# Eight closing tiles whose sums move into DRAM writes, and a second opening row on GpSimd

## The chip, the cores and the metric

The kernel runs on one core of one Trainium2 chip. Its time is the device time of one execution in microseconds; the median of three executions of the kernel before is 1081.44 us (1080.97 to 1081.83). Engines are named as the profile names them: PE (matrix multiply), PEld (its weight loads), DVE (vector), ACT (scalar), POOL (GpSimd), SP (sync, here only an issuer of DMAs).

## The reference

For 2048 tokens of width D = 576 the kernel computes `out = u + s * g`, where

```
xn = layernorm(u)                                   # per token
s  = causal convolution of xn with K + xn * D_skip  # K from an S4D state-space model, by FFT
K  = 2 Re sum_n C_n dt exp(A_n dt l)
g  = silu( gelu( layernorm(xn) @ w1 + b1 ) @ w2 + b2 )   # hidden width F = 4608
```

Everything is float32. The convolution of length 2048 is done with small transform matrices on PE.

## The kernel before, in words

PE works almost without a break on the two large products of g. Each float32 operand is split in a high and a low part, and three products (high by high, high by low, low by high) replace one. The 2048 tokens fall in two halves of 1024; token tile b (0 to 15) holds 128 tokens, b, b+16, b+32 and so on. The hidden width goes in 12 groups of 384. One "slot" is one group on one block of 512 tokens: three products of layer 1 (line 519), then gelu on ACT (L552), the high part on ACT (L555), the low part on DVE (L558), then layer 2 (L577), whose result DVE adds into the accumulator `acc` (L585). The convolution's work is laid into the gaps by a planner (`Order`) that keeps a list of steps for each line of work and traces them by estimated durations; each engine then runs its instructions in the traced order.

**Opening.** Before the first slot the order is written by hand. Token tiles 0 to 3 ("rows" in what follows) are loaded in halves from SP and ACT (L344, L345). For each of the four rows `norms` gives the steps: statistics on DVE (L372, L374), two square roots on ACT (L378, L379), a reciprocal on DVE (L382; L1163 takes rows 2 and 3 together), and `second`, the subtract-and-scale into a tile named `row` (L394). Row 0 is scaled on POOL, rows 1 to 3 on DVE. PE runs dummy products meanwhile (`warm_up`, L1132), then turns each row by five transposes (`turn_row`, L421) into three PSUM tiles. When all four rows are turned, ACT copies the transposed blocks to `XH` (L425), DVE makes the low parts `XL` (L431), and PE's first real products begin (L534). ACT also issues the loads of b1 and of a small identity (L1146, L1147) and splits the first weights (L499); DVE and POOL make their low parts (L496).

**Closing.** Tiles 8 to 11 get their last layer-2 sum in the slot before last, tiles 12 to 15 in the last slot. Tile 15 goes in two halves of 288 columns. Early, SP has loaded u of tile k+8 into `TM[k]` (`last_x`) and s into `A` (`last_s`, L639); these are `x` and `s` of `finish`. For each tile `finish` adds four or three steps: ACT takes silu (tiles 12 to 15) or tanh (8 to 11) of `acc` (L653); DVE multiplies s by it (L658, or L660 and L664); DVE adds u (`total`, L668; in the trace `w<-w,A` or `v<-v,A`); two DMAs of 64 partitions each write the sum to `out` (L671). Both go from SP; for tiles 14 and 15 the second goes from ACT, and there it stands in ACT's own order between the silus. The results of the first half of the tokens (tiles 0 to 7) are combined on the way (`combine`, L616 to L628), with DMAs from POOL.

Of the kernel before, what the change touches and what calls it, by code (L numbers as in the profile page):

```python
# [9 lines left out]
F32 = mybir.dt.float32  # L10
# [3 lines left out]
OP = mybir.AluOpType  # L14
# [3 lines left out]
L, D, N, F = 2048, 576, 128, 4608  # L18
P = 128
# [19 lines left out]
TB = 512  # L39
# [3 lines left out]
def dve(n):  # L43
    return 0.075 + 0.00104 * n
# [163 lines left out]
def step(eng, dur, fn, need=(), mark=None, cv=0, at=0.0, late=0.0, tbl=None, by=1e9):  # L208
    return dict(eng=eng, dur=dur, fn=fn, need=tuple(need), mark=mark, cv=cv, at=at, late=late, tbl=tbl, by=by)
# [3 lines left out]
def mixer_kernel(ctx, tc, u, log_a_real, a_imag, c_real, c_imag, log_dt, d_skip, w1, b1, w2, b2,  # L213
# [8 lines left out]
    def bank2(name):  # L222
        return ps.tile([P, 2, TB], F32, name=name, bufs=2 if name == "cv" else 1)
# [250 lines left out]
    def split_raw(low_on=nc.vector):  # L474
        k = state["split"]
        state["split"] += 1
        half, g, which, i = PARTS[k]
        r = RAW.pop(k)
        if which == 1:
            if i == 0 and k:  # L480
                w1_tiles()
            h, lo, r1, r2 = W[1]
            if i < KB:
                h, lo = h[:, i], lo[:, i]
                m = P
            else:
                h, lo = r1, r2[:64]
                m = 64
        else:
            if i == 0:  # L490
                W[2] = (sb.tile([P, G, D], F32R, name="w2h"), sb.tile([P, G, D], F32R, name="w2l"))
            h, lo = W[2]
            h, lo, m = h[:, i], lo[:, i], P

        def low():
            low_on.tensor_sub(lo, r[:m], h[:m].bitcast(F32))  # L496
            for _ in range(NEXT[which - 1][i]):
                load_raw()
        nc.scalar.activation(h, r, AF.Copy)  # L499
        return low  # L500
# [135 lines left out]
    def last_s(k):  # L636

        m = A2F[:, k * D:(k + 1) * D]
        nc.sync.dma_start(m, s_s[:, 8 + k, :])  # L639
        XS[8 + k] = (TM[k], m)  # L640

    TM = []

    def finish(b, c0, c1, silu, end):

        c = slice(c0, c1)
        z = acc[:, b - 8, c]
        n = c1 - c0
        T = []

        def act_z():
            T.append(sb.tile([P, D], F32, name="row", bufs=NROW)[:, c])
            nc.scalar.activation(T[0], z, AF.Silu if silu else AF.Tanh, scale=1.0 if silu else 0.5)  # L653

        def mul():
            s = XS[b][1][:, c]
            if silu:
                nc.vector.scalar_tensor_tensor(s, s, 2.0, T[0], op0=OP.mult, op1=OP.mult)  # L658
            else:
                nc.vector.tensor_mul(s, s, z)  # L660

        def mul2():
            s = XS[b][1][:, c]
            nc.vector.scalar_tensor_tensor(s, T[0], 1.0, s, op0=OP.add, op1=OP.mult)  # L664

        def total():
            x, s = XS[b]
            nc.vector.tensor_add(x[:, c], x[:, c], s[:, c])  # L668
            for y, o in enumerate(rows_at(out, b, c.start, c.stop)):
                queue = nc.scalar if end and y else nc.sync  # L670
                queue.dma_start(o, x[64 * y:64 * y + 64, c])  # L671
        st = [step("ACT", act(n), act_z, tbl="silu" if silu else "gelu"), step("DVE", dve(n), mul)]
        if not silu:
            st.append(step("DVE", dve(n), mul2))
        return st + [step("DVE", dve(n), total)]


    def params():
# [445 lines left out]
    nc.gpsimd.memset(idp, 0.0)  # L1124
    for base in (0, 1 - P):
        nc.gpsimd.affine_select(idp, idp, [[2, P]], OP.not_equal, 1.0, base=base, channel_multiplier=-1)
    q0, q1, q2 = bank2("cv"), bank2("cv"), bank2("mxb")
    qb = bank2("mxa")

    def warm_up(n):  # L1130
        for _ in range(n):
            nc.tensor.matmul(qb[:, 0], zero[:, :P], zero, start=True, stop=True)  # L1132
# [2 lines left out]
    w1_tiles()  # L1135
    na[0][0](0)

    b1r = sb.tile([P, TB], F32, name="h32", bufs=2)[:F // P, :P]
    tr = [y_transpose(0, 0, k, q) for k, q in enumerate((q0[:, 0], q1[:, 0], q2[:, 0], q0[:, 1], q1[:, 1]))]

    def turn_row(i):
        for k in (0, 3, 1, 4, 2):
            tr[k][0](i)
    lows = []
    na[0][1]()
    nc.scalar.dma_start(b1r, b1.rearrange("(k p) -> k p", p=P))  # L1146
    nc.scalar.dma_start(idt, ident)  # L1147
    na[0][2]()
    na[0][3](0, nc.gpsimd)
    turn_row(0)  # L1150
    warm_up(2)
    na[1][0](0)
    na[1][1]()
    na[2][0](0)
    lows.append(split_raw(nc.vector))
    na[2][1]()
    na[3][0](0)
    lows.append(split_raw(nc.vector))
    na[3][1]()
    na[1][2]()  # L1160
    na[1][3](0)
    turn_row(1)
    nc.vector.reciprocal(PAIR[3], PAIR[3])  # L1163
    for b in (2, 3):
        na[b][3](0)
        turn_row(b)
    nc.tensor.transpose(q2[:, 1, :F // P], b1r, idt[:F // P, :F // P])
    lows += [split_raw(nc.gpsimd), split_raw(nc.gpsimd)]
    lows[0]()
# [314 lines left out]
    for slot in range(NSLOT):  # L1484
        turn[0] = slot + 1
        n, g, tb = SEQ[slot]
        change = slot + 1 < NSLOT and SEQ[slot + 1][0] != n
        final = slot >= NSLOT - 2
        for pos in range(NPOS):
            if pos < G:  # L1490
                need = wmark(n, 1) + [("x", tb)]
                if pos == 0:
                    if slot in (mid, mid + 1):
                        x_ready(tb)
                    od.force(lambda: all(m in od.marks for m in need))

                    if slot in (3, 2 * NG + 1):
                        od.marks["x", tb] -= 2.3
                cell = []
                od.unit(lambda: cell.extend([layer1(g, tb, pos)] if slot else first_layer1(pos)),  # L1500
                        L1 if slot else L1 * (22, 6, 14)[pos] / 14, need)
                look_ahead(pos)
                for k, (a, b, c) in enumerate(cell, pos + 1 - len(cell)):
                    by = hidden_by(pos, k)
                    od.urgent.append((od.t["PE"], [step("ACT", 0.62, a, tbl="gelu", by=by[0]),
                                                   step("ACT", act(TB), b, by=by[1]),
                                                   step("DVE", dve(TB), c, mark=("h", slot, k), by=by[2])]))
                od.advance(od.t["PE"])
                if pos == G - 1 and change:
                    weigh_in(1)  # L1510
            else:
                j, terms, last, hid = l2_terms(pos - G)
                need = [wmark(n, 2)[i] for i in hid] + [("h", slot, i) for i in hid]
                if pos == G:

                    pe_turns()
                od.force(lambda: all(m in od.marks for m in need))
                if max(od.marks[m] for m in need) > od.t["PE"] + 0.3:
                    pe_turns(any_time=True)
                cell = []  # L1520
                halves = slot == NSLOT - 1 and j == 3
                od.unit(lambda: cell.append(layer2(g, tb, j, terms, last, halves)), LEN[pos], need)
                look_ahead(pos)
                if last or halves:
                    add = cell[0]
                    dh, k = (terms[0][1], 1) if halves else (0, 2)
                    done = ("acc", slot, j, dh)
                    chain = [step("DVE", dve(288 * k), lambda: add(dh, k), mark=done, by=add_by(pos, j))]
                    if final:
                        b = 8 + 4 * tb + j  # L1530
                        x = el if slot < NSLOT - 1 else od.line()
                        st = finish(b, dh * 288, (dh + k) * 288, slot == NSLOT - 1, slot == NSLOT - 1 and j > 1)
                        st[0]["need"] = (done, ("s8", b - 8))
                        x["steps"] += st
                    elif slot in GATE:
                        for d in range(2):
                            one, two = gate_store(4 * tb + j, d)
                            by = od.t["PE"] + 5.0
                            chain += [step("ACT", act(288), one, tbl="gelu", by=by), step("DVE", dve(288), two, by=by)]
                    od.urgent.append((od.t["PE"], chain))  # L1540
                if pos == NPOS - 1 and change:
                    weigh_in(2)
            for f in LATER.get((slot, pos), ()):
                f()
            od.advance(od.t["PE"])
            pe_turns(all_lines=pos in (0, 1, G + 1, G + 3, G + 5, NPOS - 1))
# [55 lines left out]
```

## Time and profile before

| | us |
|---|---|
| median of three executions | 1081.44 |
| the profiled execution's own time | 1081.68 |
| its span, first to last instruction | 1079.90 |
| first real product of PE begins (L534) | 12.95 |
| last product of PE ends (L577) | 1072.77 |
| last DVE sum ends (L668) | 1076.55 |

The profiled execution lies 0.24 us above the median, and 1.78 us of its time lie outside the span. A timeline row gives start, duration, engine, line, operation, `out<-in` by the program's tile names, shapes, and in brackets the idle time before it with the engine that ended it; `xN` merges N instructions of a kind, whose duration is then that of the whole stretch. PE's granted clock is 0.998 of full speed over the span.

### The profile page before, as it was taken

To read this page: it belongs to the slowest core of one execution; us is meant where nothing else is said; L and a number is where in the kernel's file an instruction comes from. 1 tells how busy PE (TensorE), PEld (TensorE's weight loads), DVE (VectorE), ACT (ScalarE), POOL (GpSimd) and SP (SyncE) were. 2 spreads that over 40 slices of the span, in tenths; PEclk is the share of its full clock that TensorE was granted. 3 is DMA by queue.
4 is the path that set the end of the run, shared out by engine and by line. 5 is a ranking of instruction groups with operands and counts; after the bars stand their busy time and mean duration, and the time that the engine had idled before them with its cause. 6 is when DMAs were issued, how large, how long until landed. Compare 5 with 4: busy or idle time off the path is not lost.

```text
span 1079.9 us, 27247 instructions
## 1 busy us (share of the span) xinstructions
PE 1070.8 (99%) x11471; PEld 932.4 (86%) x11471; DVE 955.2 (88%) x1535; ACT 662.2 (61%) x985; POOL 211.0 (20%) x304
## 2 busy tenths in 40 slices
PE   9999999999999999999999999999999999999997
PEld 7989899888888888888888887898888888888896
DVE  7789878999999999999999999999999997668367
ACT  6656768877658575686657657566667655234233
POOL 5669433111100020000200002000200013011231
PEclk9999999999999999999999999999999999999999
DMA  7885456643224141457322244133322436343434
GB/s 233 236 261 184 145 180 213 197 109 131 65 76 120 30 128 52 107 148 147 89 62 77 65 85 118 32 107 51 103 59 85 125 60 229 98 132 98 128 117 121
DMA packets 138570, 129.71 MB, mean 120 GB/s; under 512 B 88636, under 2 KB 109216, under 8 KB 137424
## 3 DMA queue, kind: packets, MB, share of 16 engines
q1 hardware_dynamic: 121792, 78.31, 26.8%
q0 software_dynamic: 15904, 48.70, 14.6%
q8 instruction: 90, 1.47, 0.6%
q10 hardware_dynamic: 752, 0.97, 0.3%
q14 instruction: 32, 0.26, 0.1%
HBM read 98.50 MB, written 35.19 MB: 124 GB/s over the span
## 4 chain that ended last, share of the span: by engine, by line
PE 96%; DVE 3%; issue 1%; ACT 0%; POOL 0%; ACTq 0%; DVEq 0%; POOLq 0%
PE mxb L577 21%; PE mxa L577 21%; PE mxa L519 21%; PE mxb L519 20%; PE cv L881 3%; PE cv L991 3%; PE cv L1044 2%; PE cv L953 2%; PE cv L1071 1%; PE mxa L1132 1%; DVE w2l L496 0%; PE mxa L534 0%; DVE pr L720 0%; DVE hl L558 0%; DVE A L658 0%
## 5 line engine op out<-in xcount | busy, mean ns | idle before, releaser
L577 PE MATMUL mxa<-w2h,hh 128*128 128x288 f32 x573 | 171.3, 299 | 0.3 <-DVE acc L585 0.3
L577 PE MATMUL mxb<-w2h,hh 128*128 128x288 f32 x576 | 171.6, 298 | 0.0
L577 PE MATMUL mxb<-w2h,hl 128*128 128x288 f32 x576 | 170.2, 296 | 0.0
L577 PE MATMUL mxb<-w2l,hh 128*128 128x288 f32 x576 | 169.5, 294 | 0.0
L577 PE MATMUL mxa<-w2h,hl 128*128 128x288 f32 x573 | 169.4, 296 | 0.2 <-DVE hl L558 0.2
L577 PE MATMUL mxa<-w2l,hh 128*128 128x288 f32 x573 | 168.7, 294 | 0.0
L558 DVE TENSOR_TENSOR hl<-h,hh 128x512 fp32r<-128x512 f32 x144 | 99.2, 690 | 65.2 <-ACT hh L555 64.7
L552 ACT ACTIVATE h<-mxa,b1t 128x512 f32<-128x512 f32 x73 | 50.3, 690 | 120.8 <-PE mxa L519 119.8
L781 POOL DMA_DIRECT2D par<-par_s x36 | 27.4, 762 | 480.4 <-DVE mg L824 436.4
L577 PEld LDWEIGHTS mxa<-w2h,hh 128*128 128x128 f32 x573 | 107.6, 188 | 9.8 <-issue 4.7
L577 PEld LDWEIGHTS mxb<-w2h,hh 128*128 128x128 f32 x576 | 108.1, 188 | 7.7 <-issue 3.0
L577 PEld LDWEIGHTS mxb<-w2l,hh 128*128 128x128 f32 x576 | 108.1, 188 | 0.6
L577 PEld LDWEIGHTS mxb<-w2h,hl 128*128 128x128 f32 x576 | 108.1, 188 | 0.4 <-DVE hl L558 0.2
L577 PEld LDWEIGHTS mxa<-w2h,hl 128*128 128x128 f32 x573 | 107.5, 188 | 0.6 <-DVE hl L558 0.6
L577 PEld LDWEIGHTS mxa<-w2l,hh 128*128 128x128 f32 x573 | 107.6, 188 | 0.5
L552 ACT ACTIVATE h<-mxb,b1t 128x512 f32<-128x512 f32 x71 | 49.0, 690 | 74.0 <-PE mxb L519 73.3
L555 ACT ACTIVATE hh<-h 128x512 fp32r<-128x512 f32 x144 | 91.2, 634 | 4.2
L585 DVE TENSOR_TENSOR acc<-mxa,acc 128x576 f32<-128x576 f32 x88 | 65.7, 746 | 21.3 <-PE mxa L577 20.8
L519 PE MATMUL mxa<-XH,w1h 128*128 128x512 f32 x284 | 78.9, 400 | 0.0
L519 PE MATMUL mxb<-XH,w1h 128*128 128x512 f32 x280 | 77.5, 398 | 0.0
L519 PE MATMUL mxa<-XL,w1h 128*128 128x512 f32 x284 | 76.2, 390 | 0.0
L519 PE MATMUL mxa<-XH,w1l 128*128 128x512 f32 x284 | 76.0, 389 | 0.0
(239 smaller groups left out, 2450.9 us busy)
## 6 DMA issues: line engine op xcount, KB each, us to landing
raw<-in_B_w_dram SPq DMA_DIRECT2D x75, 288.0 KB, 3.3
raw<-in_B_w_dram SPq DMA_DIRECT2D x100, 192.0 KB, 3.4
par_s<-A POOLq DMA_DIRECT2D x8, 1080.0 KB, 5.2
par<-par_s POOLq DMA_DIRECT2D x36, 240.0 KB, 3.4
f2t<-f2q SPq DMA_DIRECT2D x24, 256.0 KB, 3.5
raw<-in_B_w_dram SPq DMA_DIRECT2D x50, 96.0 KB, 3.6
u_s<-in_A_u_dram POOLq DMA_DIRECT2D x16, 288.0 KB, 4.8
xc<-xn_s SPq DMA_DIRECT2D x48, 96.0 KB, 3.8
```

Source lines behind the costliest of these rows:

```text
L519: nc.tensor.matmul(q, a, b, start=j == 0, stop=j == len(ops) - 1)
L552: nc.scalar.activation(t, q, AF.Gelu_apprx_tanh, bias=b1t[:, g * G + i:g * G + i + 1], scale=1.0)
L555: LAST[0] = nc.scalar.activation(hh[:, i], t, AF.Copy)
L558: nc.vector.tensor_sub(hl[:, i], t, hh[:, i].bitcast(F32))
L577: nc.tensor.matmul(q[:, dh, :288], a[:, i, c], b[:, i, d], start=i == 0 and k == 0, stop=i == G - 1 and k == 2)
L585: nc.vector.tensor_add(o, q[:, dh:dh + n, :288], b if first else o)
L781: nc.gpsimd.dma_start(PAR[b].rearrange("p (g i) k -> p g (i k)", g=4), dram(par_s, (b // 6 * CH + b % 6 * 4) * NPAR, [[D * NPAR, P], [24 * ...
L881: nc.tensor.matmul(q[32 * g:32 * g + 32, i // 2, i % 2 * 64:i % 2 * 64 + 64], U[:, ri, 4 * g + i, :], v[:, ri, 4 * g + i, :], start=ri == ...
L953: nc.tensor.matmul(Q1ST[i, x][g // 2][64 * f:64 * f + 64, g % 2].rearrange(order), f1t[r].rearrange("p s k -> p (s k)"), rhs(r, f), start= ...
L991: nc.tensor.matmul(Q[i][32 * q:32 * q + 32, f, 2 * ri:2 * ri + 2], m[r, 4 * i + q, 32 * ri:32 * ri + 32], A2[r, 4 * p + 2 * i + q // 2, :, ...
L1044: nc.tensor.matmul(QI[q // 2][64 * f:64 * f + 64, q % 2, i], MAT["g2t", p + i // 2][r, i % 2, ri], YS[p + i // 2][0][r, i % 2, ri, f], sta ...
L1071: nc.tensor.matmul(Q[f][32 * e:32 * e + 32, t], g1t[r], A2[r, k:k + 2, 1].rearrange("p i d r -> p i r d"), start=True, stop=True, skip_gro ...
```

## The change

The sum of tiles 8 to 14 leaves DVE. SP writes u of the tile from `TM[k]` to `out` as soon as s has been loaded, two DMAs a tile (14 in all). The last product of a tile (`product`) now writes over the u tile in SBUF, and POOL issues two DMAs that add it to what `out` holds (`accum_op`). Seven of DVE's nine sums are gone. Tile 15 keeps its two sums; ACT issues only the last of its four stores, where ACT issued three of the six stores of tiles 14 and 15 before. A new condition (`need`) puts the first half's product of tile 15 behind the sum of the second half into `acc`.

In the opening POOL scales row 1 too, right after row 0; the reciprocals of rows 2 and 3 are separate; rows are turned in the order 0, 2, 1, 3; one dummy product instead of two stands after row 0. POOL issues the loads of b1 and of the identity, now 36 by 36 instead of 128 by 128, ahead of its scalings.

```
         nc.sync.dma_start(m, s_s[:, 8 + k, :])
         XS[8 + k] = (TM[k], m)
+        if k < 7:
+            for y, o in enumerate(rows_at(out, 8 + k, 0, D)):
+                nc.sync.dma_start(o, TM[k][64 * y:64 * y + 64])
...
+        def product(a, k, op, b2):
+            x, s = XS[b]
+            o = s[:, c] if end else x[:, c]
+            nc.vector.scalar_tensor_tensor(o, a, k, b2, op0=op, op1=OP.mult)
+            if not end:
+                for y, r in enumerate(rows_at(out, b, c0, c1)):
+                    nc.gpsimd.dma_start(r, o[64 * y:64 * y + 64], accum_op=OP.add)
...
-                queue = nc.scalar if end and y else nc.sync
+                queue = nc.scalar if c1 == D and y else nc.sync
...
-        return st + [step("DVE", dve(n), total)]
+        return st + [step("DVE", dve(n), total)] * end
...
+    nc.gpsimd.dma_start(b1r, b1.rearrange("(k p) -> k p", p=P))
+    nc.gpsimd.dma_start(idt[:F // P, :F // P], ident[:F // P, :F // P])
...
-    nc.scalar.dma_start(b1r, b1.rearrange("(k p) -> k p", p=P))
-    nc.scalar.dma_start(idt, ident)
     na[0][2]()
     na[0][3](0, nc.gpsimd)
     turn_row(0)
-    warm_up(2)
+    warm_up(1)
...
+    na[1][2]()
+    na[1][3](0, nc.gpsimd)
...
-    na[1][3](0)
-    turn_row(1)
-    nc.vector.reciprocal(PAIR[3], PAIR[3])
-    for b in (2, 3):
-        na[b][3](0)
-        turn_row(b)
+    na[2][2]()
+    na[2][3](0)
+    turn_row(2)
+    turn_row(1)
+    na[3][2]()
+    na[3][3](0)
+    turn_row(3)
...
-                        st = finish(b, dh * 288, (dh + k) * 288, slot == NSLOT - 1, slot == NSLOT - 1 and j > 1)
+                        st = finish(b, dh * 288, (dh + k) * 288, slot == NSLOT - 1, slot == NSLOT - 1 and j == 3)
                         st[0]["need"] = (done, ("s8", b - 8))
+                        if halves and not dh:
+                            st[1]["need"] = (("acc", slot, j, 1),)
```

The order on DVE in the opening, from the reciprocal of row 0 to the first weight split, stood so before:

```order
L382 RECIPROCAL U_88<-U_88 128x2
L372 BN_STATS st_171<-acc_87 128x6 x2
L374 BN_AGGR U_88<-st_171 128x2
L372 BN_STATS st_177<-acc_87 128x6 x2
L374 BN_AGGR U_88<-st_177 128x2
L372 BN_STATS st_184<-acc_87 128x6 x2
L374 BN_AGGR U_88<-st_184 128x2
L382 RECIPROCAL U_88<-U_88 128x2
L394 TENSOR_SCALAR row_192<-acc_87,U_88 128x576
L1163 RECIPROCAL U_88<-U_88 128x2x2
L394 TENSOR_SCALAR row_200<-acc_87,U_88 128x576
L394 TENSOR_SCALAR row_207<-acc_87,U_88 128x576
```

and stands so now (`st_...` of the second, third and fourth statistics are rows 1, 2 and 3):

```order
L382 RECIPROCAL U_88<-U_88 128x2
L372 BN_STATS st_170<-acc_87 128x6 x2
L374 BN_AGGR U_88<-st_170 128x2
L372 BN_STATS st_176<-acc_87 128x6 x2
L374 BN_AGGR U_88<-st_176 128x2
L382 RECIPROCAL U_88<-U_88 128x2
L372 BN_STATS st_186<-acc_87 128x6 x2
L374 BN_AGGR U_88<-st_186 128x2
L382 RECIPROCAL U_88<-U_88 128x2
L394 TENSOR_SCALAR row_194<-acc_87,U_88 128x576
L382 RECIPROCAL U_88<-U_88 128x2
L394 TENSOR_SCALAR row_207<-acc_87,U_88 128x576
```

The reciprocal of row 1 moved ahead of row 3's statistics, and one scaling of three left DVE (POOL has it behind row 0's).

The order on DVE at the end, from the sum of tile 12 into `acc`, stood so before (`w` and `v` are u tiles, `A_81` the s tiles, `cv` the last half of tile 15):

```order
L585 TENSOR_TENSOR acc<-mxb,acc 128x576
L585 TENSOR_TENSOR acc<-mxa,acc 128x576
L658 SCALAR_TENSOR_TENSOR A_81<-A_81,row 128x576
L668 TENSOR_TENSOR w<-w,A_81 128x576
...
L585 TENSOR_TENSOR acc<-mxb,acc 128x576
L668 TENSOR_TENSOR w<-w,A_81 128x576
L585 TENSOR_TENSOR acc<-mxa,acc 128x288
L658 SCALAR_TENSOR_TENSOR A_81<-A_81,row 128x576
L585 TENSOR_TENSOR acc<-cv,acc 128x288
L668 TENSOR_TENSOR v<-v,A_81 128x576
L658 SCALAR_TENSOR_TENSOR A_81<-A_81,row 128x288
L668 TENSOR_TENSOR v<-v,A_81 128x288
...
```

and stands so now (L661 is the product, L678 the sum that is left):

```order
L585 TENSOR_TENSOR acc<-mxb,acc 128x576
L585 TENSOR_TENSOR acc<-mxa,acc 128x576
L661 SCALAR_TENSOR_TENSOR w<-A_81,row 128x576 x2
L585 TENSOR_TENSOR acc<-mxb,acc 128x576
L585 TENSOR_TENSOR acc<-mxa,acc 128x288
L661 SCALAR_TENSOR_TENSOR v<-A_81,row 128x576
L585 TENSOR_TENSOR acc<-cv,acc 128x288
L661 SCALAR_TENSOR_TENSOR A_81<-A_81,row 128x288
L678 TENSOR_TENSOR v<-v,A_81 128x288
...
```

The three sums of 576 columns are gone; a product and a sum of 288 columns follow twice after the last sum from `cv`.

The end of ACT's order, from the silu of tile 12, stood so before:

```order
L653 ACT_TABLE_LOAD
L653 ACTIVATE row<-acc 128x576 x3
L653 ACTIVATE row<-acc 128x288
L671 DMA out_dram<-v 64x576
L653 ACTIVATE row<-acc 128x288
L671 DMA out_dram<-v 64x288 x2
```

and stands so now:

```order
L656 ACT_TABLE_LOAD
L656 ACTIVATE row<-acc 128x576 x3
L656 ACTIVATE row<-acc 128x288 x2
L681 DMA out_dram<-v 64x288
```

No DMA stands between the last two silus any more.

## Rows read from the trace of the kernel before

**Rows 1.** Page: the chain of work that ended last, by engine.
```profile
PE 96%; DVE 3%; issue 1%; ACT 0%; POOL 0%; ACTq 0%; DVEq 0%; POOLq 0%
```

**Rows 2.** Timeline of the last stretch, PE and ACT: start, duration, instruction.
```profile
1070.11 0.30 PE L577 MATMUL mxb<-w2h,hl 128*128 128x288 f32 x1
...
1071.65 0.69 ACT L653 ACTIVATE row<-acc 128x576 f32<-128x576 f32 x1 [2.11 <-DVE acc L585]
...
1072.48 0.29 PE L577 MATMUL cv<-w2h,hl 128*128 128x288 f32 x1
...
1074.38 0.54 ACTq L671 DMA_DIRECT2D out_dram<-v  x1
...
1075.12 0.45 ACT L653 ACTIVATE row<-acc 128x288 f32<-128x288 f32 x1 [1.93 <-DVE A L658]
```

**Rows 3.** Timeline of the last stretch, DVE.
```profile
1070.86 0.75 DVE L585 TENSOR_TENSOR acc<-mxb,acc 128x576 f32<-128x576 f32 x1
...
1072.20 0.45 DVE L585 TENSOR_TENSOR acc<-mxa,acc 128x288 f32<-128x288 f32 x1
1072.56 0.75 DVE L658 SCALAR_TENSOR_TENSOR A<-A,row 128x576 f32<-128x576 f32 x1
1073.23 0.45 DVE L585 TENSOR_TENSOR acc<-cv,acc 128x288 f32<-128x288 f32 x1
...
1075.60 0.46 DVE L658 SCALAR_TENSOR_TENSOR A<-A,row 128x288 f32<-128x288 f32 x1 [0.39 <-ACT row L653]
1076.09 0.46 DVE L668 TENSOR_TENSOR v<-v,A 128x288 f32<-128x288 f32 x1
```

**Rows 4.** Line L671: SP's last issues (ns min/median/max, first and last start); landing.
```profile
L671 SPq DMA_DIRECT2D out_dram<-v x3: 467/467/468, 1074.4 to 1076.6; - x3
...
DMA to landing us min/median/max: 2.0/2.4/3.5
```

**Rows 5.** Timeline of the opening, DVE.
```profile
5.79 0.17 DVE L382 RECIPROCAL U<-U 128x2 f32<-128x2 f32 x1 [0.55 <-ACT U L379]
...
7.36 0.82 DVE L372 BATCH_NORM_STATS2 st<-acc 128x6 f32<-128x288 f32 x2 [0.21 <-DMA acc<-in_A_u_dram]
8.21 0.21 DVE L374 BATCH_NORM_AGGREGATE U<-st 128x2 f32<-128x12 f32 x1
...
10.64 1.07 DVE L394 TENSOR_SCALAR row<-acc,U 128x576 f32<-128x576 f32 x2
```

**Rows 6.** Timeline of the opening, POOL, PE and ACT.
```profile
6.07 2.29 POOL L394 TENSOR_SCALAR row<-acc,U 128x576 f32<-128x576 f32 x1 [3.93 <-DVE U L382]
...
11.33 0.60 PE L421 MATMUL cv<-idp,row 128*128 128x128 f32 x4
...
11.88 0.60 PE L421 MATMUL cv<-idp,row 128*128 128x128 f32 x4
...
12.30 1.09 ACT L425 ACTIVATE XH<-cv 128x512 fp32r<-128x512 f32 x2 [1.07 <-PE cv L421]
```

**Rows 7.** Timeline of the last stretch, POOL: its last four issues.
```profile
1066.73 2.13 POOL L628 DMA_DIRECT2D out_dram<-row  x4 [10.92 <-DVE row L625]
```

**Rows 8.** Page: POOL's loads from DRAM; KB each, us to landing.
```profile
par<-par_s POOLq DMA_DIRECT2D x36, 240.0 KB, 3.4
```

**Rows 9.** Line L404: landing of POOL's stores of a whole row tile.
```profile
DMA to landing us min/median/max: 2.4/3.5/6.6
```

**Rows 10.** Timeline of the last weight load (SP) and its slot's first layer-2 product.
```profile
1030.28 0.33 SPq L459 DMA_DIRECT2D raw<-in_B_w_dram  x1
...
1044.03 0.29 PE L577 MATMUL mxa<-w2h,hh 128*128 128x288 f32 x1
```

**Rows 11.** Timeline around 88 us: a POOL scaling beside DVE scalings.
```profile
86.54 0.57 DVE L394 TENSOR_SCALAR row<-w,U 128x576 f32<-128x576 f32 x1
...
86.81 2.80 POOL L403 TENSOR_SCALAR w<-w,U 128x576 f32<-128x576 f32 x1
...
88.03 1.06 DVE L394 TENSOR_SCALAR row<-v,U 128x576 f32<-128x576 f32 x2
```

More of the change, by code (lines that the diff above doesn't have):

```diff
@@ L657, in mul @@
             if silu:
-                nc.vector.scalar_tensor_tensor(s, s, 2.0, T[0], op0=OP.mult, op1=OP.mult)
+                product(s, 2.0, OP.mult, T[0])
             else:
@@ L662, in mul2 @@
         def mul2():
-            s = XS[b][1][:, c]
-            nc.vector.scalar_tensor_tensor(s, T[0], 1.0, s, op0=OP.add, op1=OP.mult)
+            product(T[0], 1.0, OP.add, XS[b][1][:, c])
         def total():
@@ L1126, in mixer_kernel @@
         nc.gpsimd.affine_select(idp, idp, [[2, P]], OP.not_equal, 1.0, base=base, channel_multiplier=-1)
+    b1r = sb.tile([P, TB], F32, name="h32", bufs=2)[:F // P, :P]
+    nc.gpsimd.dma_start(b1r, b1.rearrange("(k p) -> k p", p=P))
+    nc.gpsimd.dma_start(idt[:F // P, :F // P], ident[:F // P, :F // P])
     q0, q1, q2 = bank2("cv"), bank2("cv"), bank2("mxb")
@@ L1136, in mixer_kernel @@
     na[0][0](0)
-    b1r = sb.tile([P, TB], F32, name="h32", bufs=2)[:F // P, :P]
     tr = [y_transpose(0, 0, k, q) for k, q in enumerate((q0[:, 0], q1[:, 0], q2[:, 0], q0[:, 1], q1[:, 1]))]
@@ L1154, in mixer_kernel @@
     na[2][0](0)
+    na[2][1]()
+    na[1][2]()
+    na[1][3](0, nc.gpsimd)
     lows.append(split_raw(nc.vector))
-    na[2][1]()
     na[3][0](0)
+    na[3][1]()
     lows.append(split_raw(nc.vector))
-    na[3][1]()
-    na[1][2]()
-    na[1][3](0)
+    na[2][2]()
+    na[2][3](0)
+    turn_row(2)
     turn_row(1)
-    nc.vector.reciprocal(PAIR[3], PAIR[3])
-    for b in (2, 3):
-        na[b][3](0)
-        turn_row(b)
+    na[3][2]()
+    na[3][3](0)
+    turn_row(3)
     nc.tensor.transpose(q2[:, 1, :F // P], b1r, idt[:F // P, :F // P])
```

## The prediction

> **What bounds the kernel now.** I read the chain of work that ended last first: 96% of it is PE [rows 1]. From its first real product to its last, which ends at 1072.48 + 0.29 = 1072.77 [rows 2], PE is the whole chain, and the change leaves the products as they are. So only the two ends can change the time: what happens before the first product, and the 1079.90 - 1072.77 = 7.13 us behind the last. For these I read the timelines, engine by engine.
>
> At the end the reader is to see two queues that are late [rows 2, 3]. The last bank is full at 1072.77, but DVE turns to it at 1073.23, since it has been in tile 14's product from 1072.56. DVE is done with it at 1073.68, yet the silu of that half starts on ACT only at 1075.12: in ACT's order the store of tile 14 stands ahead, and this waits for DVE's sum and goes at 1074.38. The product follows at 1075.60, the sum at 1076.09 to 1076.55. From there to the end of the span it is 3.35 us: the issues start at 1076.6, a store lands 2.4 us after its issue starts [rows 4], and about 0.9 us close the program.
>
> In the opening the last transpose counts. Row 3 is scaled at the end of the pair 10.64 to 11.71 [rows 5], PE begins to turn it at 11.88, 0.55 after row 2, ACT copies from 12.30 [rows 6], and PE's first real product waits for that copy.
>
> **The end, part by part.** The sums of tiles 12, 13 and 14 go from DVE, and with them the ACT store. Each step below uses gaps of these rows: a product started 0.36 after an independent instruction of 288 columns (1072.20 to 1072.56), a sum 0.49 after its product (1075.60 to 1076.09), ACT 0.04 after DVE (1070.86 + 0.75 to 1071.65) [rows 2, 3]; I take 0.04 between the other engines too. PE's pace is (1072.48 - 1070.11) / 18 = 0.132 per product.
>
> - Tile 14's bank is full at 1070.41. DVE, which stood in tile 13's product until 1070.86, is free: sum into `acc` 1070.45 to 1071.20, silu 1071.24 to 1071.93, product 1071.97 to 1072.72. The bank of tile 15's first half is full nine products before the end, at 1071.58; its sum runs at 1071.62, its silu 1072.11 to 1072.56.
> - DVE is then free for the last bank: 1072.81 to 1073.26, and silu 1073.30 to 1073.75, without the store ahead of it.
> - DVE goes on with the first half's product at 1073.17, sum 1073.66 to 1074.12, the second half's product at 1074.02 (0.36 after the sum's start; its silu is ready), sum 1074.51 to 1074.97. This is 1.58 before 1076.55.
> - ACT's store starts at once. SP has the first half's two stores ahead of its last one: issues of 0.47 from 1074.15, so the last starts at 1075.09 or a little after where it was 1076.6: 1.46 earlier by 1075.12. SP's store is the later of the two, so the end gains **1.46**.
>
> What stands against it are POOL's additions. Tiles 12 and 13 are done in time; tile 14's product ends at 1072.72, POOL issues in 2.13 / 4 = 0.53 each [rows 7], the second from 1073.30. No row shows an adding DMA. It can land no sooner than the fastest store, 2.0 [rows 4], and with a load and a store one behind the other, 3.4 [rows 8] + 2.4 = 5.8; the longest landing of a plain store of POOL is 6.6 [rows 9]. Hidden is what lands within 4.2 us: 1073.30 + 4.2 + 0.9 = 1078.4, where the other stores end too (1074.97 + 3.35 + 0.12). I take 3.5, the median of POOL's stores of a tile twice this size, so it costs nothing.
>
> SP's 14 early stores of u follow its loads of s, the first twelve of them ahead of the last weight load. With about 0.5 an issue they push it by 6 us; it went at 1030.28, and PE first uses its group at 1044.03 [rows 10], so 13.7 us cover it, less its landing and its split. On POOL four additions of tiles 8 and 9 push the last loads of tiles 6 and 7 by 2.1, and four of tiles 10 and 11 follow; POOL then idled 10.92 us [rows 7], which covers both. The tanh of tile 10 now waits for POOL's stores of tiles 3 to 5, and the gelu behind it on ACT is needed only three layer-1 products later.
>
> **The opening, part by part.** DVE loses one scaling (0.5), and row 3 is ready sooner: reciprocal of row 1 behind row 2's statistics (8.42), row 3's statistics end about 9.65, row 2 scaled 9.8 to 10.4, reciprocal, row 3 scaled 10.5 to 11.1 in place of 11.71. But row 1 is now POOL's. Row 2's statistics wait for their data until 7.36 and end at 8.42; the reciprocal 8.45 to 8.62 [rows 5]; POOL follows 0.11 after it, as 5.96 to 6.07 for row 0. POOL's scaling takes 2.29 with nothing beside it [rows 6], so row 1 is ready at 8.73 + 2.29 = 11.02. Beside DVE's scalings it took 2.80: it began at 86.81, one DVE scaling ran until 87.11 and two from 88.03 [rows 11]. That is 0.51 for two and a part, 0.2 each. Here two fall into it, so 11.02 + 0.40 = 11.42.
>
> PE begins to turn a row 0.11 after it is ready (10.64 + 0.58 to 11.33); row 3 comes 0.55 after row 1; ACT 0.42 after that [rows 6]: 11.42 + 0.11 + 0.55 + 0.42 = 12.50 where it was 12.30. So the opening **loses 0.20**, and what follows shifts as a whole, since it hangs on that copy. Bounds: without the stretch 12.10, a gain of 0.20; with the full 0.51 12.61, a loss of 0.31. ACT's two issues go and its roots come sooner, which is worth nothing, since ACT idles 1.07 us ahead of 12.30 [rows 6]. POOL's two issues lie in the 3.93 us in which it waited for row 0 [rows 6]. The dummy product that goes lay ahead of row 1's turn and frees nothing now.
>
> **Sum.** 1081.68 - 1.46 + 0.20 = 1080.42 for an execution like the profiled one; the median lies 0.24 lower: **1080.2 us**.
>
> **The rivals.**
>
> *POOL is not slowed.* Row 1 at 11.02, the opening gains 0.20: 1079.8. For it: bn_stats beside row 0 cost POOL nothing (2.29). Against it: the 2.80 of [rows 11].
>
> *The additions land last (the other side).* If an addition reads what `out` holds before it writes, it lands after 5.8 us: 1073.30 + 5.8 + 0.9 = 1080.0, against 1079.90 before, and with 0.20 of the opening 1081.8: slower by 0.3, with 6.6 us by 1.1 (1082.6). It decides from 4.2 us on, and it makes the kernel slower from 5.5. For it: loads take longer than stores, and an addition is both. Against it: the data is small, and reading and writing may overlap across its 64 rows. The Trainium skill ("Collectives: The Full Stack", section "The bandwidth ceiling: the fold count and why AG ≠ RS ≠ AR") says that an add in the DMA path is slow because it reads two sources, not because of the add; no run here shows it yet.
>
> *DVE waits for POOL.* If POOL's scaling, which starts first, held DVE's two scalings back until 11.02, row 2 would be ready at 11.60 and row 3, with its reciprocal, at 12.3; the copy comes at 12.3 + 0.11 + 0.42 = 12.85, a loss of 0.55: 1080.5. In [rows 11] DVE's pair took 1.06 though POOL had begun 1.2 us before, as 1.07 in the opening with POOL idle [rows 5], and it was POOL that took longer. The Trainium skill ("SBUF — State Buffer", section "Who interferes with whom") says that the engine which issues first holds the shared pair of ports for its whole instruction and the other blocks; by that rule this rival would be the forecast, and the trace does not agree.
>
> **How the numbers follow.** Forecast 56%, POOL not slowed 15%, additions last 18% (in a third of it slower than before), DVE waits 6%, something I do not see 5%. The forecast's own range is 1079.7 to 1080.8. The range for 8 in 10 takes the gain of both ends at its best (-1.58 - 0.20, less 0.3 for the scatter of the executions: 1079.3) and the addition at 5.8: 1079.3 to 1081.8. A measurement can tell about 0.2%, 2.2 us, from no change. All my cases but the worst additions lie within it: faster by more than 0.2% needs a further 0.4 us beyond both best ends, 13%; within 0.2% 82%; slower by more than 0.2% needs additions that land after 7.6 us, 5%.
>
> **What would show it.** In the changed kernel's timeline: row 1's scaling on POOL longer than 2.29 and ending near 11.4, PE idle between row 2 and row 1, the first copy at 12.5. At the end: the sum from `cv` at 0.04 after PE's last product, the silu 0.5 later, the last sum about 2.2 after PE's end instead of 3.78. The prediction is wrong if the additions' landings end the span (landing above 4.2), if the first copy comes before 12.1, or if PE's products between the two ends take another time than now.

## The result, and the profile after

The changed kernel takes 1084.18 us (median of 10 executions, 1083.63 to 1084.95), the kernel before 1081.41 us beside it: a ratio of 1.0026, 95% interval 1.0018 to 1.0034. The prediction was 1080.2 us (1079.3 to 1081.8), so the change is 2.8 us slower where 1.2 us faster was forecast. The profiled execution took 1084.33 us, its span 1082.6 us [before: 1081.68 and 1079.9].

The share of the chain by engine, from the page of the changed kernel, answers to [rows 1]:

```profile
PE 92%; DVE 3%; DMA 2%; issue 1%; ACT 1%; POOL 0%; SPq 0%; DVEq 0%; ACTq 0%; POOLq 0%
```

PE is still nearly everything, and this view hides the loss: the chain goes back from the last *busy* instruction, DVE's last sum, and what comes behind that does not stand in it. (The 4% that PE has less are pieces before 90 us that the view follows through loads, POOL and ACT. PE was busy meanwhile, 46.84 of the 47 us from 13 to 60 (it starts at 13.16) and 9.95 of the 10 from 60 to 70, where it was 47.00 and 10.00 before.) So the timeline of the end is read first, engine by engine (start, duration, engine, line; answers to [rows 2, 3, 4]):

```profile
1072.52 0.75 DVE L661 SCALAR_TENSOR_TENSOR v<-A,row 128x576 f32<-128x576 f32 x1
...
1073.01 0.29 PE L577 MATMUL cv<-w2h,hl 128*128 128x288 f32 x1
1073.33 0.46 DVE L585 TENSOR_TENSOR acc<-cv,acc 128x288 f32<-128x288 f32 x1
1073.56 1.85 POOL L664 DMA_DIRECT2D out_dram<-v  x2
1073.71 0.45 DVE L661 SCALAR_TENSOR_TENSOR A<-A,row 128x288 f32<-128x288 f32 x1
1073.83 0.44 ACT L656 ACTIVATE row<-acc 128x288 f32<-128x288 f32 x1 [0.69 <-DVE acc L585]
...
1074.68 1.97 SPq L681 DMA_DIRECT2D out_dram<-v  x3
1075.06 0.46 DVE L678 TENSOR_TENSOR v<-v,A 128x288 f32<-128x288 f32 x1
1075.54 0.52 ACTq L681 DMA_DIRECT2D out_dram<-v  x1
```

DVE and ACT do what the prediction said: PE ends at 1073.30, DVE follows 0.03 later, the last sum ends at 1075.52, 2.22 behind PE, where it was 3.78. Yet the span ends 9.30 behind PE's last product (1082.6 - 1073.30) where it was 7.13. The DMAs show why. First POOL's additions, by their line (durations min/median/max, first and last start; then issue to landing):

```profile
L664 POOL DMA_DIRECT2D out_dram<-w x4: 863/1316/1770, 1070.3 to 1072.0; - x4
L664 POOL DMA_DIRECT2D out_dram<-v x2: 1007/1162/1316, 1073.6 to 1074.1; - x2
...
DMA to landing us min/median/max: 3.3/4.7/5.6
```

and the issues that lie in single stretches (the first addition, the last one, then the plain stores of tile 15; the last column is issue to landing):

```profile
out_dram<-w POOLq DMA_DIRECT2D x1, 144.0 KB, 3.3
...
out_dram<-v POOLq DMA_DIRECT2D x1, 144.0 KB, 5.6
...
out_dram<-v SPq DMA_DIRECT2D x3, 72.0 KB, 4.4
...
out_dram<-v ACTq DMA_DIRECT2D x1, 72.0 KB, 4.5
```

Four additions start within 1.7 us, 0.55 apart. The first of the six lands at 1070.3 + 3.3 = 1073.6, the last at 1074.1 + 5.6 = 1079.7: one in 1.2 us, twice as slow as they are issued, so a backlog forms. The plain stores of tile 15 land after 4.2 to 4.7 us, where the last two took 2.0 and 2.2 before. The stretches behind PE's end in the kernel before (the last columns are PE's granted clock, the DMA engines' share and GB/s):

```profile
1073.00:1076.00 3.00, 0.00 (x0) 0.00 (x0) 2.58 (x6) 0.63 (x2) 0.00 (x0) 0.97 0.59 133
1076.00:1079.00 3.00, 0.00 (x0) 0.00 (x0) 0.51 (x2) 0.00 (x0) 0.00 (x0) 0.50 0.56 162
```

and in the changed one:

```profile
1073.00:1076.00 3.00, 0.29 (x3) 0.06 (x1) 2.38 (x6) 0.58 (x2) 2.41 (x3) 1.00 1.03 129
1076.00:1079.00 3.00, 0.00 (x0) 0.00 (x0) 0.00 (x0) 0.00 (x0) 0.00 (x0) 0.62 0.96 199
```

The 16 DMA engines, a little over half busy before, are full (1.03, 0.96) until 1079; in the run e3 below, which has the same transfers without the adding, the shares are 0.65 and 0.17. The Trainium skill ("DMA: Bandwidth & Descriptors", section "Issuing engines are not separate DMA queues") says that transfers issued by different engines run on the same 16 DMA engines and interleave; the trace agrees, by these shares and by the 4.4 us.

Last, the instructions that close the program (min/median/max in ns, first and last start), in the kernel before:

```profile
L1598 POOLq DRAIN  x3: 46/103/3731, 1068.1 to 1079.6; - x3
L1598 SPq DRAIN  x3: 7/7/7, 1079.1 to 1079.4; - x3
```

and in the changed one:

```profile
L1612 POOLq DRAIN  x3: 46/103/7730, 1074.0 to 1082.3; - x3
L1612 SPq DRAIN  x3: 7/7/7, 1080.4 to 1082.0; - x3
```

SP drains first when its waits for all landings are over: at 1079.1 before, 1080.4 now. POOL's long drain begins with its last issue: before, it ended at 1068.1 + 3.73 = 1071.8, long past; now it ends at 1074.0 + 7.73 = 1081.7, 1.3 after SP's waits and 2.0 after the last addition landed. The span ends 0.8 to 0.9 behind the later of the two in both kernels.

So the 2.17 us lost behind PE are: last sum -1.56; last issue +0.36 (SP starts it at 1075.9, 0.38 behind the sum, since its three issues queue; 0.02 before); landing of the last plain store and SP's waits +2.0 (4.5 behind the issue, 2.5 before); POOL's drain +1.3. These make 2.1; the rest is rounding and the close (0.87 instead of 0.80 behind the later of the two).

The timeline of the opening of the changed kernel, DVE, then POOL, then ACT (answers to [rows 5, 6]):

```profile
6.38 0.82 DVE L372 BATCH_NORM_STATS2 st<-acc 128x6 f32<-128x288 f32 x2 [0.40 <-DMA acc<-in_A_u_dram]
7.96 0.82 DVE L372 BATCH_NORM_STATS2 st<-acc 128x6 f32<-128x288 f32 x2 [0.51 <-DMA acc<-in_A_u_dram]
...
10.26 0.58 DVE L394 TENSOR_SCALAR row<-acc,U 128x576 f32<-128x576 f32 x1
...
10.95 0.80 DVE L394 TENSOR_SCALAR row<-acc,U 128x576 f32<-128x576 f32 x1
...
9.15 2.29 POOL L394 TENSOR_SCALAR row<-acc,U 128x576 f32<-128x576 f32 x1 [0.76 <-DMA raw<-in_B_w_dram]
...
12.51 0.60 ACT L425 ACTIVATE XH<-cv 128x512 fp32r<-128x512 f32 x1 [0.56 <-PE cv L421]
```

The first copy comes at 12.51 (predicted 12.50, before 12.30), but by another road: row 2's data are 0.6 late, POOL starts row 1 at 9.15 instead of 8.73 and is *not* slowed; it is DVE's scaling of row 3 that takes 0.80, where row 2's took 0.58. It ends at 11.75, 0.31 behind POOL's scaling (9.15 + 2.29 = 11.44), but PE turned to row 3 only at 12.10, so that cost nothing: the copy follows POOL's scaling by 1.07 (1.08 predicted).

### The profile page after: what moved, and what is told of

It reads as the page before. It is cut to its first block, busy times and chain, and to the rows that moved or that the text cites. A ratio compares the mean times of both kernels' runs of the same rounds, so it can differ in the third digit from the quotient of the medians.

```text
span 1082.6 us, 27267 instructions
## 1 busy us (share of the span) xinstructions
PE 1069.9 (99%) x11470; PEld 931.4 (86%) x11470; DVE 950.8 (88%) x1528; ACT 661.8 (61%) x985; POOL 226.6 (21%) x321
## 4 chain that ended last, share of the span: by engine, by line
PE 92%; DVE 3%; DMA 2%; issue 1%; ACT 1%; POOL 0%; SPq 0%; DVEq 0%; ACTq 0%; POOLq 0%
PE mxb L577 20%; PE mxa L577 20%; PE mxa L519 20%; PE mxb L519 19%; PE cv L891 3%; PE cv L1001 3%; PE cv L1054 2%; PE cv L963 2%; PE cv L1081 1%; DMA w<-in_A_u_dram 1%; DMA acc<-in_A_u_dram 1%; POOL w L403 0%; DMA raw<-in_B_w_dram 0%; DVE w2l L496 0%; PE mxa L534 0%
```

## The experiments

All were timed in 10 or 11 executions against the kernel before on the same chip. "Last sum", "SP" (its waits over), "POOL" (its drain over) and "end" are us behind the end of PE's last product in the profile, read as above.

| run | median | minus before | 95% interval of the ratio | last sum | SP | POOL | end |
|---|---|---|---|---|---|---|---|
| before | 1081.41 | | | 3.78 | 6.3 | -1.0 | 7.13 |
| changed | 1084.18 | +2.77 | 1.0018-1.0034 | 2.22 | 7.1 | 8.4 | 9.30 |
| e1 closing part only | 1083.65 | +2.10 | 1.0013-1.0031 | 2.21 | 7.6 | 8.5 | 9.33 |
| e2 opening only | 1081.89 | +0.34 | 0.9995-1.0013 | 3.75 | 6.2 | -0.9 | 7.08 |
| e3 plain stores (u left out) | 1081.09 | -0.46 | 0.9988-1.0005 | 2.22 | 4.9 | 5.7 | 6.45 |
| e4 add 8-11 | 1081.64 | +0.09 | 0.9994-1.0012 | 3.28 | 6.4 | -0.2 | 7.23 |
| e5 add 14 only | 1082.38 | +1.37 | 1.0004-1.0023 | 2.62 | 6.4 | 7.2 | 8.02 |
| e6 POOL sums 14 | 1082.04 | +1.03 | 1.0002-1.0019 | 3.74 | 7.5 | 5.0 | 8.34 |
| e7 POOL sums 12-14 | 1082.53 | +1.52 | 1.0007-1.0025 | 4.03 | 7.8 | 5.3 | 8.62 |
| e8 DVE sums, SP three | 1080.89 | -0.12 | 0.9992-1.0009 | 3.29 | 6.2 | -1.0 | 7.09 |
| e9 stores shared | 1081.72 | +0.45 | 0.9995-1.0013 | 3.29 | 6.8 | -1.0 | 7.62 |
| e10 e9 + add 12 | 1081.69 | +0.42 | 0.9995-1.0013 | 3.28 | 6.8 | 3.7 | 7.59 |
| e11 e9 + add 12, 13 | 1081.60 | +0.33 | 0.9993-1.0011 | 2.85 | 6.4 | 5.9 | 7.16 |
| e12 row 1 on POOL only | 1081.47 | +0.20 | 0.9994-1.0012 | 3.76 | 6.2 | -0.9 | 7.13 |
| e13 queue in order | 1080.72 | -0.40 | 0.9987-1.0005 | 3.29 | 5.9 | -1.0 | 6.67 |
| e14 e13, last on POOL | 1081.98 | +0.86 | 0.9999-1.0017 | 3.30 | 6.1 | 7.2 | 7.97 |
| e15 two loads only | 1081.12 | 0.00 | 0.9991-1.0009 | 3.73 | 6.2 | -0.9 | 7.09 |

In every row the end is 0.8 to 0.9 behind the later of SP and POOL.

**e1 and e2: the two halves of the change.** Edit: the opening, or all else, as in the kernel before.

> The opening of the kernel before, the closing part of the changed one. My theory now: the changed kernel loses in two places, 0.5 us before PE's last product (0.2 at the first copy, 0.2 where PE waits for a low part near 63.8 us, 0.1 later) and 2.2 us behind it. Then this one shows the first copy at 12.3, no wait of PE near 63.8, PE's last product ending near 1072.9, and the end of the span still 9.3 us behind that: 1083.8 us. Rival: the opening is worth nothing, and the 0.5 us are scatter of the executions: 1084.2 us.

> The opening of the changed kernel, the closing part of the kernel before. If the opening is what delays PE: first copy at 12.5, the wait near 63.8 us there again, PE's last product ending near 1073.2, the end 7.13 us behind it as before: 1081.8 us. Rival: no change against before, 1081.4 us, since the later copy is caught up somewhere.

The closing part alone gives the loss: end 9.33, +2.10. The opening alone is not told from no change. The "0.2 near 63.8 us" and "0.1 later" of my expectation don't hold: from the first copy to PE's last product it is 1072.77 - 12.30 = 1060.47 us before and 1060.79 in the changed kernel, but 1059.75 in e14 and 1061.08 in e15, with the same products between; that much is scatter.

**e3: the adding itself.** Against the changed kernel:

```diff
-nc.gpsimd.dma_start(r, o[64 * y:64 * y + 64], accum_op=OP.add)
+nc.gpsimd.dma_start(r, o[64 * y:64 * y + 64])
```

> The changed kernel with POOL's 14 stores writing the product instead of adding it (the sum with u is left out in tiles 8 to 14). Theory 'the adding is the cost': the additions leave POOL's queue one per 1.2 us though they are issued every 0.55 us, so that a backlog forms, which also holds up the last plain stores (4.2 to 4.7 us to landing) and POOL's drain. Without the adding they land about 2 us after their issue, the last store about 2.2 us after its own, and the span ends 5.7 to 6.0 us behind PE's last product instead of 9.3: about 1080.8 us. Rival 'POOL as issuer': what counts is that POOL issues so late and has to be drained; then POOL's drain ends about as late, and the time is within 0.5 us of 1084.2.

POOL's line in e3, with its landings:

```profile
L664 POOL DMA_DIRECT2D out_dram<-w x4: 527/527/529, 1069.4 to 1070.9; - x4
L664 POOL DMA_DIRECT2D out_dram<-v x2: 527/527/527, 1072.6 to 1073.1; - x2
...
DMA to landing us min/median/max: 2.3/2.7/2.9
```

and the drains that close e3:

```profile
L1612 POOLq DRAIN  x3: 46/103/4907, 1073.1 to 1078.5; - x3
L1612 SPq DRAIN  x3: 7/7/7, 1077.2 to 1078.3; - x3
```

The same issues in the same order, the same bytes written, no adding (so u is missing from the output of tiles 8 to 14): the landings fall from 3.3-5.6 to 2.3-2.9, the plain stores' from 4.4 to 2.2, and the end from 9.30 to 6.45. The adding costs 2.85 us. What makes it slow is not taken apart here: POOL's issues are longer too, 0.86 to 1.77 us with the adding and 0.53 without. The rival keeps a part: POOL's drain (1073.1 + 4.9 = 1078.0) still ends 0.8 behind SP's waits, which is why 5.7 to 6.0 was not reached.

**e4 and e5: which additions.** Against the changed kernel (e4; e5 has `b != 14`; the early stores of u go with the additions, and the condition that gives ACT the last store alone is adapted):

```diff
-st = finish(b, ..., slot == NSLOT - 1, slot == NSLOT - 1 and j == 3)
+st = finish(b, ..., slot == NSLOT - 1, b >= 12)
```

> The changed kernel with only tiles 8 to 11 added in DRAM; the sums of tiles 12 to 14 are on DVE again and go out by SP, and ACT issues the last store alone. Theory 'the adding is the cost': nothing of POOL is late, the stores land after 2.0 to 2.5 us. DVE has tile 14's sum (0.7) ahead of tile 15's products, so the last sum is 2.9 after PE's last product (2.2 in the changed kernel, 3.78 before), and the end 6.3 behind it: 1081.2 us. Rival: the gain on DVE came from the sums that went, not from the order of ACT's queue: last sum 3.6 or more after PE's last product, 1082 us.

> The changed kernel with only tile 14 added in DRAM; tiles 8 to 13 are summed on DVE and stored by SP, as before. It tells whether the backlog of six additions or the last pair alone costs the time. Theory 'backlog': the two land after 3.3 and 4.5 us, as the first two of the changed kernel's rows did, the plain stores are hardly slowed, and only POOL's drain, about 2 us behind the last landing, holds the end: about 8.0 us behind PE's last product (9.3 in the changed kernel, 7.13 before), 1082.8 us. Rival 'hidden but for the backlog', as my prediction had it: 5.6 to 6 us behind PE's last product, 1080.5 us.

In e4 nothing is lost and nothing won: last sum 3.28 instead of 2.9, and SP's five stores in a row delay the last one, which starts 0.8 behind its sum. In e5 there is no backlog of six: the two additions land after 3.2 and 4.2 us, and still the end is 8.02. This is no clean test of the 4.2 that my prediction called hidden, for the sums of tiles 12 and 13 are back on DVE, so that the second addition starts 1.4 behind PE's last product (0.5 in the prediction) and lands 5.6 behind it. SP's stores of tile 15 and the drains:

```profile
out_dram<-v SPq DMA_DIRECT2D x3, 72.0 KB, 3.5
...
L1612 POOLq DRAIN  x3: 46/103/5865, 1073.8 to 1080.2; - x3
L1612 SPq DRAIN  x3: 7/7/7, 1078.9 to 1079.9; - x3
```

POOL's ends at 1079.7, 1.6 after the last addition landed (1073.9 + 4.2) and 0.8 after SP's waits, and sets the end, as the theory said. Its "hardly slowed" is wrong: beside two additions the plain stores of tile 15 take 3.5 and 3.6 us instead of 2.0 to 2.1, and SP's waits are over no sooner than before (6.4, 6.3) though the last sum comes 1.2 sooner.

**e8, e9, e13: what the closing part is worth without additions.** All sums on DVE, old opening. e13:

```diff
+if b == 15 and late:                    # tile 14's second store, behind the last silu
+    nc.scalar.dma_start(*late.pop())
 ...
+if b == 14 and y:
+    late.append((o, r))
+else:
+    (nc.scalar if b == 15 and y else nc.sync).dma_start(o, r)
```

In e9 the two lines with `late.pop()` come behind the loop, in e8 there too and SP issues three of tile 15's four stores.

> No addition in DRAM, the opening of the kernel before, all sums on DVE; only ACT's queue is put in order (its store of tile 14 behind the last silu) and the last stores shared out between SP and ACT. It tells how much of the closing gain needs the sums to go from DVE. DVE has tile 14's sum ahead of tile 15's products: last sum 3.1 after PE's last product, the end 6.5 behind it: 1080.8 us. Rival: the order of ACT's queue is worth nothing by itself: 7.1 behind, 1081.4 us.

> No addition in DRAM, the opening of the kernel before, all sums on DVE, ACT's store of tile 14 behind the last silu, and the stores of tile 15 shared as before, one of each pair on SP and one on ACT (in the run e8 SP issued three in a row, 0.5 to 0.6 each, and the last started 0.37 after its sum). Theory: DVE's work sets the last sum, 3.3 after PE's last product as in e8, and the last stores now start at once: the end 6.65 behind PE's last product, 0.5 under the kernel before of the same call. Rival: the issues were not what was late, 7.1 behind, no difference.

> e9 with ACT's store of tile 14 put ahead of its two stores of tile 15 (in e9 it came between them, and the last store started 0.65 late). No addition in DRAM, all sums on DVE, the opening of the kernel before. Theory: what the closing part is worth without the additions is the order of ACT's queue alone: last sum 3.3 after PE's last product, both last stores issued at once, the end 6.65 behind, 0.5 us under the kernel before of the same call, which a comparison of medians can hardly tell from none. Rival: the end stays 7.1 behind.

e8 and e9 missed by a queue of my own making: their last store starts 0.4 and 0.6 behind the last sum. (The 7.09 of e8 is its rival's number for that reason.) e13 hits: 6.67 for 6.65. Its tail:

```profile
1073.55 0.74 DVE L676 TENSOR_TENSOR v<-v,A 128x576 f32<-128x576 f32 x1
1073.67 0.44 ACT L654 ACTIVATE row<-acc 128x288 f32<-128x288 f32 x1 [0.53 <-DVE acc L585]
...
1074.33 0.54 ACTq L678 DMA_DIRECT2D out_dram<-v  x1
```

The last silu comes 0.94 behind PE's last product (1072.73), not 2.35, but DVE has tile 14's sum ahead, so only 0.49 of it reaches the last sum. Of the kernels that compute every sum e13 is the fastest: clearly under the changed kernel, but its -0.40 us to the kernel before is within what can't be told from none.

**e14: POOL's drain by itself.** e13 with one plain store moved:

```diff
-(nc.scalar if b == 15 and y else nc.sync).dma_start(o, r)
+(nc.gpsimd if c0 and y else nc.scalar if b == 15 and y else nc.sync).dma_start(o, r)
```

> e13 with one of the two last stores issued by POOL, a plain store. It measures POOL's drain by itself. Theory: POOL's drain ends about 2 us behind the landing of its last transfer (1.7 to 2.4 in the profiles so far), where SP's wait ends 0.25 behind a landing; so the end comes 1.4 to 2.1 us later than in e13 though the store lands as soon. Rival: the drain only looked late because the additions were; then e14 ends with e13.

POOL's store in e14 (KB, issue to landing in us):

```profile
out_dram<-v POOLq DMA_DIRECT2D x1, 72.0 KB, 2.1
```

The drains that close e14:

```profile
L1613 POOLq DRAIN  x3: 46/103/3606, 1075.3 to 1079.4; - x3
L1613 SPq DRAIN  x3: 7/7/7, 1077.8 to 1079.2; - x3
```

The store lands at 1075.3 + 2.1 = 1077.4, no slower than on ACT; POOL's drain ends at 1078.9, 1.5 later, and the end is 7.97 instead of 6.67: 1.30 for this alone, and 0.86 more over before than e13's -0.40 makes 1.26 by the medians. A little under the 1.4 expected, but not the rival's nothing.

**e10 and e11: additions early enough.** e9 with `b not in (12,)`, or `(12, 13)`, as `end`.

> As e9, with tile 12 alone added in DRAM. Theory: an addition is free where its landing and POOL's drain, 2 us behind it, end before the last store: the two land about 1.8 us after PE's last product, POOL's drain ends near 4, and the last store lands near 5. DVE is rid of one sum (0.67): last sum 2.6 after PE's last product, the end 6.0 behind it, 1.1 us under the kernel before of the same call. Rival: the additions slow the stores beside them by 1 us again, so that nothing is left of the 0.67: no better than e9.

> As e10, with tiles 12 and 13 added in DRAM. Theory: the fourth addition lands 4.3 us after PE's last product, as in e1, and POOL's drain ends 2 us later: the end 7.2 behind, no gain on the kernel before though DVE is rid of two sums. Rival: only tile 14's additions were too late, the end 5.6 to 6 behind.

e10's theory fails on DVE, not on the DMAs: POOL's drain is over at 3.7, but the last sum stays at 3.28, because DVE now waits 0.39 for tile 14's silu ahead of its product; the rival's slowed stores are seen only at tile 13 (3.6 to 3.9 us). e11 has the expected number (7.16; the fourth addition lands 4.4 behind PE) by another road: the drain is over at 5.9, ahead of SP's waits (6.4). Tile 14's first store takes 3.7 us and the next 2.8, and as in e9 and e10 the last store starts 0.6 behind the last sum. Neither was run with the queue of e13, so whether an early addition is worth something there stays open.

**e6 and e7: sums on GpSimd.**

```diff
+nc.gpsimd.tensor_add(x[:, c], x[:, c], o)
```

> No addition in DRAM. The opening of the kernel before; tile 14's sum is a GpSimd instruction, its two stores go on ACT behind the last silu, SP has the other last stores; tiles 8 to 13 as before. Theory: the closing gain of the changed kernel is real and only the additions hide it. POOL's sum takes 1.5 us (1.02 for 384 columns at L496), DVE is free for the last bank, last sum 2.4 after PE's last product, the end 5.9 behind it: about 1080.3 us. Rival: POOL's sum slows DVE's chain beside it or is itself late, so that the end is 7 us behind as before: 1081.4 us.

> As the one before, with the sums of tiles 12 and 13 on GpSimd too, so that DVE's tail is that of the changed kernel. Theory: last sum 2.2 after PE's last product, the end 5.7 behind it: about 1080.1 us. Rival: three sums of 1.5 us on POOL run into each other, tile 14's is late and its stores end the span: 6.5 us behind or more, 1080.9 us or later.

Both theories failed. e6's rival has the cause (POOL's sum slows DVE) at a larger price. e7's rival has the size but not the cause: tile 14's sum on POOL waited for DVE's product, which had stood still beside POOL's sum of tile 13, and it is not tile 14's stores that come last. In e6's timeline, the product of tile 15's first half, 0.45 us elsewhere, and POOL's sum beside it:

```profile
1072.97 1.57 DVE L659 SCALAR_TENSOR_TENSOR A<-A,row 128x288 f32<-128x288 f32 x1
...
1072.83 1.40 POOL L661 TENSOR_TENSOR v<-v,A 128x576 f32<-128x576 f32 x1 [4.60 <-PE cv L577]
```

DVE's product ends 0.3 after POOL's sum: it stood still beside it. The sum from `cv`, which reads one operand of PSUM, was done in 0.45 between 1072.61 and 1073.06. In e7 the products of tiles 14 and 15 took 1.61 and 1.55 beside POOL's sums, instead of 0.75 and 0.45. The Trainium skill ("SBUF — State Buffer", section "Who interferes with whom") says that a DVE instruction with two SBUF inputs contends with a GpSimd instruction that reads SBUF; here the trace agrees. But this explains only why the last sum is no earlier than before (3.74 and 4.03; 3.78). That the end is later by 1.2 and 1.5 is again a queue: SP issues all four stores of tile 15, and the last starts at 1077.0 in both, 1.1 and 1.2 behind the last sum. GpSimd sums with the queue of e13 were not run.

**e12 and e15: the two parts of the opening.**

> The opening of the changed kernel but for the two small loads, which ACT issues as before; the closing part of the kernel before. Theory: the later first copy (12.4 on the mean of the five profiles with the new opening, 12.1 with the old one) comes from row 1 on POOL, whose 2.29 us start only after row 2's statistics: first copy at 12.4, 0.3 us slower than before of the same call. Rival: the two early loads are what delays the rows' data; then the first copy is at 12.1 and the time that of before.

> The kernel before with nothing changed but that POOL issues the two small loads of the opening. Theory: these loads, now 4 to 5 us earlier, share the queues with the rows' data: row 2's statistics start at 7.7 instead of 7.3, the first copy at 12.4 instead of 12.0, 0.3 us slower than before of the same call. Rival: they cost nothing and row 1 on POOL was the loss: first copy near 12.0.

First copy at 12.06 and at 11.93: in one profile each, neither part shows the copy later than the ten profiles with the old opening (mean 12.02, 11.77 to 12.30), and neither moves the time. The five profiles with the whole new opening have 12.35 (12.08 to 12.56), but these ranges overlap, so a loss of 0.3 us is not shown. What is shown is the path. In e12:

```profile
10.42 0.88 DVE L394 TENSOR_SCALAR row<-acc,U 128x576 f32<-128x576 f32 x1
...
8.70 2.29 POOL L394 TENSOR_SCALAR row<-acc,U 128x576 f32<-128x576 f32 x1 [0.30 <-DMA raw<-in_B_w_dram]
```

In all six profiles with row 1 on POOL (e12 and the five) the first copy comes 1.07 to 1.08 behind the end of that scaling, which takes 2.28 to 2.30 each time; so the copy is as late as POOL starts, 8.70 (e12) to about 9.2. And in all six DVE's scaling of row 3 ends 0.30 to 0.32 behind POOL's (it takes 0.80 to 1.04): it waits for POOL, at no cost, while row 2's, beside the same POOL scaling, takes 0.58. Why the one waits and the other does not stays open, and so does what makes POOL start later in some profiles than in others.

## Why the prediction was wrong

- **The DVE and ACT side of the end: right.** Sum from `cv` 0.03 after PE (0.04 said), silu 0.5 later, last sum 2.22 (2.2). A small miss lies behind it: SP's issues start 0.61 apart, not 0.47, so the last store starts 0.38 behind its sum instead of 0.15. e13 shows that 0.5 of the gain belongs to the order of ACT's queue, the rest to the sums that left DVE.
- **The step that failed: "Hidden is what lands within 4.2 us ... I take 3.5 ... so it costs nothing."** The price of one addition was fair: the first lands after 3.3. But it is the price of one transfer [rows 9], and three things were not in the step. (1) It counted tile 14's additions alone, with those of tiles 12 and 13 "done in time"; but six additions issued 0.55 apart land 1.2 apart, the last after 5.6; by the prediction's own sign (a landing above 4.2) it was wrong. (2) I asked when the additions land, not what they do to the plain stores beside them: 4.2 to 4.7 us instead of 2.0 to 2.5. (3) A POOL transfer is not done when it lands: POOL's drain takes another 1.5 to 2.1 us, and POOL had been idle for so long before the end [rows 7] that the 0.9 "to close the program" never held it. e14 shows this term by itself: 1.30. With it, and with the second addition starting 0.83 behind PE's last product instead of 0.53, the limit for being hidden was near 2.6 and not 4.2 (an estimate, 4.2 - 1.3 - 0.3); e3 bears it out, where even a plain POOL store of 2.8 left the drain 0.8 behind SP's waits.
- **The rival "additions land last" had the right place, but neither the cause nor the price.** Its 5.8 is a load and a store one behind the other in each addition; the first addition landed after 3.3, and the 5.6 of the last came of the backlog. With that 5.6 its sum says 7.0 behind PE's last product (0.53 + 5.6 + 0.9); it was 9.30: 0.30 by the later issue, 2.0 by the drain. The points from which it "decides" (4.2, and 5.5 for slower) were both too late for the same reason, so its chance for slower by over 0.2%, tied to 7.6 us, was far too small. The Trainium skill ("Collectives: The Full Stack", section "The bandwidth ceiling: the fold count and why AG ≠ RS ≠ AR"), cited there, says it of a collective, the ReduceScatter: slow because the add needs two source reads, not because of the add. e3 shows that an adding DMA is slower (3.3 to 5.6 us against 2.3 to 2.9); no run here separates its reading from its sum.
- **SP's early stores, POOL's loads, the tanh that waits: hidden, as said.** From 1030 to 1060 PE has 30.00 us busy in both kernels.
- **The opening: the path right, the size by accident.** 12.50 said, 12.51 found, and the 1.08 from POOL's row 1 to the copy holds in six profiles. But POOL's scaling took 2.29, not 2.69, and started at 9.15, not 8.73, as the rows' data came later: two misses of 0.4 that cancel. "POOL is not slowed" was right in its premise and wrong in its price, since it took the data's time from the profile before. "DVE waits for POOL" happened to one scaling of two: row 2's was not held (0.58), row 3's was (0.80, until 0.31 behind POOL's end), where it cost nothing. [rows 11] had spoken against any such wait.
- **The sum.** Forecast -1.46 and +0.20. Measured in the two profiles: +2.17 behind PE's last product, +0.21 at the first copy and +0.32 between, of which the last is scatter and the opening's part not told from it: 2.70, against 2.77 in the medians.

## What to carry to other kernels

A transfer is hidden only if its landing, the transfers that it slows, and the drain of the engine that issued it all end before the last store has landed; ask for all three, and keep the last microseconds of a program free of GpSimd's DMAs. A gain on the compute engines behind the last product is worth nothing until the issue queues let the last stores go at once: e8, e9 and e13 differ by nothing else. Where the chain view ends at a busy instruction, read the closing waits and drains too.

## What the runs showed of the hardware that was not expected

- POOL's drain at the end of the program ended 1.5 (e14), 1.6 (e5), 2.0 (changed kernel) and 2.1 us (e3) after POOL's last transfer had landed.
- An adding transfer of 144 KB: 3.3 us for the first, one per 1.2 us in a row; the same store without adding 2.3 to 2.9.
- DVE's product of two SBUF operands stood still beside GpSimd's sum of two (1.57 for 0.45 us). Its scaling of row 3, of one operand, ended 0.30 to 0.32 us behind GpSimd's scaling of row 1 in six profiles (0.80 to 1.04 for 0.58), while row 2's scaling, the statistics (0.82 for two) and the sum with a PSUM operand (0.45) were not slowed.
- Issues back to back on one queue cost more than single ones: 0.54, 0.80 and 0.77 for three on ACT in e9, 0.50 to 0.54 for the three of the kernel before.
